# A two-layer SiLU network on one core: tile 0 of the first tokens transposed alone, slab 1 loaded from ScalarE's queue

## The chip, the core and the metric

The kernel runs on one core of one Trainium2 chip. The metric is device microseconds from the start to the end of one execution; a result is the median of several executions. Every duration below comes from the times, or from one profiled execution of the kernel.

The profile names the engines PE (TensorE, matrix products), PEld (TensorE's weight loads, which overlap the products), ACT (ScalarE), DVE (VectorE), POOL (GpSimd) and SP (SyncE). A "q" behind a name (SPq, ACTq) stands for that engine's instruction sequencer, which also issues DMAs.

## The reference

```python
B, S, D, F = 1, 2048, 640, 1728
x: (B, S, D)   w1: (D, F)   w2: (F, D)      # all bf16

def reference(x, w1, w2):
    h = jnp.einsum("bsd,df->bsf", x, w1)
    h = _silu(h)
    out = jnp.einsum("bsf,fd->bsd", h, w2)
    return out
```

## The kernel before

**Layout.** The first product needs the contraction dimension D on the 128 partitions. So `xT` holds x transposed: 5 tiles of D (`DT` = 5, 128 partitions each) by 2048 tokens. The transposing is done by the DMA (`dma_start_transpose`), and all transposes are issued from SP's queue. `w1s` holds w1 in 5 slabs, slab k being the 128 rows of D that belong to tile k. F = 1728 is 13 blocks of 128 columns (`FT` = 13) and a rest of 64. Tokens are worked in 4 chunks of 512 (`SCH`).

**First chunk.** In the first chunk data are still arriving, so the loops are turned inside out: for k = 0 to 4, for each of the first 8 blocks of F (`NO` = 8, one PSUM bank each), one product of slab k with tile k (lines 197 to 211). Each such product is a pair of matmuls of 64 output rows each (`step`, line 183) that run side by side in two halves of the array. PE's instruction stream thus waits in turn for tile 0 and slab 0 (line 199), the second part of slab 0 before block 5 (`NA` = 5, line 202), slab and tile 1, 2, 3 (line 205), slab and tile 4 (line 208). After that come blocks 8 to 12 of this chunk (lines 221 to 228, waiting for `ld_rest` and `ld_rest2`, the other columns of w1), the chunks 1 to 3 (lines 229 to 235, each waiting for its transposed tokens `ld_xc`), and the second product.

**Before the data.** PE starts with products of zeros: `first_dummies` (line 135) issues 13 products of 128 x 128 by 256 columns and then one pair of 64-row halves. They write PSUM that the first real product overwrites, and depend only on a memset of `z`.

**The order of the loads.** `early` (line 96) puts an instruction ahead of the barrier at the program's start, at the end of what its engine has there already; the order of the calls is thus the order on each queue. Before the change:

- SP: tiles 0 and 1 of chunk 0 in one transposing DMA (line 123); columns of blocks 5 to 7 of slab 0 (`ld_w1b`, line 148); slab 1; slab 2; tile 2; slab 3; tiles 3 and 4 in one DMA; slab 4; `ld_rest`; `ld_rest2`. Behind the barrier follow 15 transposing DMAs of one tile each for the chunks 1 to 3, and then w2.
- ScalarE: columns of blocks 0 to 4 of slab 0 (line 124, 160 KB), then the warm-up (lines 142 to 146): one SiLU on a small tile that makes the engine load its function table. It waits for POOL's memset of `warm`.

A slab's 8 blocks are 256 KB. The transposing DMAs are records of line 93 or 163, the loads of line 88, the matmuls of line 175 (and 132 for the products of zeros).

Of the kernel before, what the change touches and what calls it, by code (L numbers as in the profile page):

```python
# [9 lines left out]
def bass_standalone__dense_activation_silu__prompt_kernel(  # L10
# [13 lines left out]
    P = 128  # L24
# [5 lines left out]
    SCH = 512  # L30
# [8 lines left out]
    pe, act, dve, pool, sp = nc.tensor, nc.scalar, nc.vector, nc.gpsimd, nc.sync  # L39

    with ExitStack() as es:
# [18 lines left out]
        def sem(name):  # L60
            s = es.enter_context(nc.semaphore(name))
            count[s.name if hasattr(s, "name") else name] = 0
            return [s, 0]

        def tick(ins, s, n=1):
            ins.then_inc(s[0], n)
            s[1] += n
            return (s, s[1])

        def wait(eng, *points):  # L70
            for pt in points:
                if pt is None:
                    continue
                s, v = pt
                key = (id(eng), id(s))
                if seen.get(key, 0) < v:
                    eng.wait_ge(s[0], v)
                    seen[key] = v
# [6 lines left out]
        def load(eng, out_ap, in_ap):  # L85
            s = sem(f"s_ld{n_dma[0]}")
            n_dma[0] += 1
            return tick(eng.dma_start(out=out_ap, in_=in_ap), s, 16)

        def turned(c0, c1, k0, k1):  # L90
            s = sem(f"s_tr{n_dma[0]}")
            n_dma[0] += 1
            return tick(sp.dma_start_transpose(
                out=xT[:, k0:k1, c0:c1], in_=xf[c0:c1, k0 * P:k1 * P]), s, 16)

        ET = mybir.EngineType

        def early(emit, engine, arrived=True):
            n = len(nc.main_func.blocks[0].instructions)
            r = emit()  # L100
            lst = nc.main_func.blocks[0].instructions
            new = lst[n:]
            del lst[n:]
            at = next(
                i for i, ins in enumerate(lst)
                if ins.opcode == ("EventSemaphore" if arrived else "Drain") and ins.engine == engine
            )
            lst[at:at] = new
            return r
# [8 lines left out]
        def slab(eng, k, f0=0, f1=NO):  # L118
            return load(eng, w1s[:, k, f0 * P:f1 * P], w1_v[:, k, f0 * P:f1 * P])

        ld_w1 = {}
        ld_t = {}
        ld_t[0] = ld_t[1] = early(lambda: turned(0, SCH, 0, 2), ET.SP, False)
        ld_w1[0] = early(lambda: slab(act, 0, 0, NA), ET.Activation, False)
        p_z = early(lambda: tick(dve.memset(z[:, :], 0.0), s_dve), ET.DVE, False)  # L125

# [2 lines left out]
        def dummies(n, w):  # L129
            for _ in range(n):  # L130
                for c0 in range(0, P, w):
                    pe.matmul(ps[c0:c0 + w, 3, 0:HB], lhsT=z[:, 0:w], rhs=z[:, :],  # L132
                              start=True, stop=True)

        def first_dummies():
            wait(pe, p_z)
            dummies(13, P)
            dummies(1, HC)

        p_warm = early(lambda: tick(pool.memset(warm[:, :], 0.0), s_pool), ET.Pool, False)  # L140
# [4 lines left out]

        early(warm_up, ET.Activation, False)

        ld_w1b = early(lambda: slab(sp, 0, NA, NO), ET.SP, False)
        ld_w1[1] = early(lambda: slab(sp, 1), ET.SP, False)
        ld_w1[2] = early(lambda: slab(sp, 2), ET.SP, False)  # L150
        ld_t[2] = early(lambda: turned(0, SCH, 2, 3), ET.SP, False)
        ld_w1[3] = early(lambda: slab(sp, 3), ET.SP, False)
        ld_t[3] = ld_t[4] = early(lambda: turned(0, SCH, 3, DT), ET.SP, False)
        ld_w1[4] = early(lambda: slab(sp, 4), ET.SP, False)
# [42 lines left out]
        def opening():  # L197
            first_dummies()
            wait(pe, ld_t[0], ld_w1[0])
            for ft in range(NO):  # L200
                if ft == NA:
                    wait(pe, ld_w1b)
                part(0, ft, 0, SCH, start=True)
            for k in range(1, DT - 1):
                sweep(k, 0, SCH, ld_w1[k], ld_t[k])
# [202 lines left out]
```

## Time and profile before

| what | before |
|---|---|
| median of 3 runs | 124.61 us (124.4 to 124.67) |
| span of the profiled execution, first to last instruction | 123.84 us |
| PE busy | 121.3 us, 98% of the span |
| weight loads busy | 58.9 us |
| ACT busy | 38.8 us |
| DVE busy | 6.9 us |
| HBM read, written | 4.51 MB, 2.62 MB |
| granted TensorE clock in every stretch | 1.00 |

The span is 0.77 us shorter than the median time; that much lies around the first and the last recorded instruction. A busy PE is not a PE at its best rate: how fast it goes is read from the distance between the starts of successive products. A DMA has three moments: the issue (an instruction of SPq or ACTq with a duration of its own), the packets that the 16 DMA engines move, and the landing, when the last of the 16 semaphore increments has arrived. A row "x1, 3.8" among the DMA issues means 3.8 us from the start of the issue to the landing.

### The profile page before, as it was taken

Reading aid. Unit: us, or ns where it says so; the run is one execution under the profiler, and the core shown is the slowest. Engines: PE = TensorE matmul, PEld = TensorE weight load, DVE = VectorE, ACT = ScalarE, POOL = GpSimd, SP = SyncE. Lnnn points to the kernel's source line nnn. Section 1 sums busy time; section 2 is a strip of 40 time slices with the busy share of each in tenths; the row PEclk is TensorE's granted clock in tenths of the full one; section 3 lists DMA queues with packets and bytes.
Section 4 is the critical chain, followed back from the end, with each engine's and each line's share of the span. In section 5 each row is a group of like instructions: output and inputs, shape, how many; then the busy total and the mean of one; then the engine's idle time right before and its main releaser. Section 6 shows DMA issues by size and latency. Waiting matters only on the chain.

```text
span 123.8 us, 2298 instructions
## 1 busy us (share of the span) xinstructions
PE 121.3 (98%) x1056; PEld 58.9 (48%) x1057; DVE 6.9 (6%) x11; ACT 38.8 (31%) x67; POOL 0.3 (0%) x5
## 2 busy tenths in 40 slices
PE   8999999999999999999999999999999999999993
PEld 5345545545545545545544444444444444444452
DVE  0000000000000000000000022002200300222001
ACT  4000985555555555555530011001100200110110
POOL 0000000000000000000000000000000000000000
DMA  6999974554894000000000004302200220023112
GB/s 138 239 246 331 138 86 91 100 77 107 214 394 157 0 0 0 3 5 0 0 0 5 0 0 101 74 0 105 107 0 5 106 106 0 5 106 116 53 66 82
DMA packets 19625, 10.42 MB, mean 84 GB/s; under 512 B 13728, under 2 KB 19104, under 8 KB 19616
## 3 DMA queue, kind: packets, MB, share of 16 engines
q1 hardware_dynamic: 19472, 10.11, 34.1%
q10 hardware_dynamic: 144, 0.16, 0.6%
q8 instruction: 8, 0.13, 0.5%
q14 instruction: 1, 0.01, 0.0%
HBM read 4.51 MB, written 2.62 MB: 58 GB/s over the span
## 4 chain that ended last, share of the span: by engine, by line
PE 95%; DMA 3%; ACT 0%; issue 0%
PE ps L175 95%; DMA xT<-in_x_dram 3%; ACT o_sb L256 0%
## 5 line engine op out<-in xcount | busy, mean ns | idle before, releaser
L175 PE MATMUL ps<-xT,w1s 128*64 128x512 bf16 x540 | 59.6, 384 | 0.1
L175 PE MATMUL ps<-w2s,hT 64*128 64x512 bf16 (+3 forms) x376 | 46.0, 369 | 0.2 <-issue 0.2
L175 PEld LDWEIGHTS ps<-xT,w1s 128*64 128x64 bf16 x540 | 30.0, 111 | 29.6 <-issue 1.2
L179 ACT ACTIVATE hT<-ps 128x512 bf16<-128x512 f32 x52 | 30.0, 607 | 29.9 <-PE ps L175 29.9
L175 PEld LDWEIGHTS ps<-w2s,hT 64*128 64x128 bf16 (+1 forms) x377 | 21.0, 95 | 24.2 <-issue 0.2
L256 ACT CAST o_sb<-ps 128x512 bf16<-128x512 f32 (+1 forms) x9 | 5.0, 551 | 41.5 <-PE ps L175 41.5
L175 PE MATMUL ps<-hT,w2s 64*128 64x512 bf16 x104 | 11.7, 376 | 0.0
L175 PEld LDWEIGHTS ps<-hT,w2s 64*128 64x128 bf16 x104 | 5.0, 94 | 6.3 <-issue 0.4
L254 DVE CAST o_sb<-ps 128x512 bf16<-128x512 f32 (+1 forms) x8 | 5.4, 675 | 40.5 <-PE ps L175 40.5
L254 DVE CAST oT<-ps 128x512 bf16<-128x512 f32 x2 | 1.4, 692 | 74.2 <-PE ps L175 74.2
L256 ACT CAST oT<-ps 128x512 bf16<-128x512 f32 x2 | 1.2, 586 | 10.6 <-PE ps L175 10.6
L132 PE MATMUL ps<-z 128*128 128x256 bf16 (+1 forms) x15 | 3.3, 419 | 0.4 <-DVE z L125 0.4
L175 PE MATMUL ps<-w2t,hTt 64*128 64x512 bf16 (+2 forms) x17 | 2.9, 363 | 0.0
L132 PEld LDWEIGHTS ps<-z 128*128 128x128 bf16 (+1 forms) x15 | 1.9, 142 | 1.5 <-issue 0.4
L179 ACT ACTIVATE hTt<-ps 128x512 bf16<-128x512 f32 x2 | 1.2, 598 | 1.0 <-PE ps L175 1.0
L144 ACT ACT_TABLE_LOAD x1 | 1.3, 1283 | 0.5 <-issue 0.5
L175 PEld LDWEIGHTS ps<-w2t,hTt 64*128 64x128 bf16 x17 | 0.9, 94 | 1.1
L175 PE MATMUL ps<-hTt,w2t 64*128 64x512 bf16 x4 | 0.8, 376 | 0.0
L175 PEld LDWEIGHTS ps<-hTt,w2t 64*128 64x128 bf16 x4 | 0.2, 94 | 0.2
L144 ACT ACTIVATE warm<-warm 128x32 f32<-128x32 f32 x1 | 0.2, 229 | 0.0
L125 DVE MEMSET z<- 128x128 uint32 x1 | 0.2, 165 | 0.2 <-issue 0.2
L140 POOL MEMSET warm<- 128x32 f32 x1 | 0.1, 125 | 0.0
(4 smaller groups left out, 0.4 us busy)
## 6 DMA issues: line engine op xcount, KB each, us to landing
out_dram<-o_sb SPq DMA_DIRECT2D x15, 160.0 KB, 1.8
w2s<-in_w_dram SPq DMA_DIRECT2D x1, 1120.0 KB, 6.1
w1s<-in_w_dram SPq DMA_DIRECT2D x4, 256.0 KB, 4.1
w2s<-in_w_dram SPq DMA_DIRECT2D x1, 960.0 KB, 8.2
w1s<-in_w_dram SPq DMA_DIRECT2D x1, 560.0 KB, 7.0
w1s<-in_w_dram SPq DMA_DIRECT2D x1, 320.0 KB, 5.8
xT<-in_x_dram SPq DMA_TRANSPOSE x18, 3.7
w1s<-in_w_dram ACTq DMA_DIRECT2D x1, 160.0 KB, 2.7
```

Source lines behind the costliest of these rows:

```text
L125: p_z = early(lambda: tick(dve.memset(z[:, :], 0.0), s_dve), ET.DVE, False)
L132: pe.matmul(ps[c0:c0 + w, 3, 0:HB], lhsT=z[:, 0:w], rhs=z[:, :], start=True, stop=True)
L140: p_warm = early(lambda: tick(pool.memset(warm[:, :], 0.0), s_pool), ET.Pool, False)
L144: act.activation(out=warm[:, :], in_=warm[:, :], func=ACT.Silu)
L175: return pe.matmul(o, lhsT=l, rhs=r, start=start, stop=stop, skip_group_check=shared)
L179: r = tick(act.activation(out=out_ap, in_=in_ap, func=ACT.Silu), s_act)
L254: r = tick(dve.tensor_copy(out=out_ap, in_=in_ap), s_dve)
L256: r = tick(act.copy(out=out_ap, in_=in_ap), s_act)
```

## The change

```diff
-        ld_t[0] = ld_t[1] = early(lambda: turned(0, SCH, 0, 2), ET.SP, False)
+        ld_t[0] = early(lambda: turned(0, SCH, 0, 1), ET.SP, False)
         ld_w1[0] = early(lambda: slab(act, 0, 0, NA), ET.Activation, False)
...
         def first_dummies():
             wait(pe, p_z)
-            dummies(13, P)
+            dummies(11, P)
             dummies(1, HC)
...
         early(warm_up, ET.Activation, False)
 
+        ld_w1[1] = early(lambda: slab(act, 1), ET.Activation, False)
+
         ld_w1b = early(lambda: slab(sp, 0, NA, NO), ET.SP, False)
-        ld_w1[1] = early(lambda: slab(sp, 1), ET.SP, False)
+        ld_t[1] = ld_t[2] = early(lambda: turned(0, SCH, 1, 3), ET.SP, False)
         ld_w1[2] = early(lambda: slab(sp, 2), ET.SP, False)
-        ld_t[2] = early(lambda: turned(0, SCH, 2, 3), ET.SP, False)
         ld_w1[3] = early(lambda: slab(sp, 3), ET.SP, False)
```

SP's first DMA transposes tile 0 alone. Tiles 1 and 2 follow in one DMA behind the second part of slab 0. The load of slab 1 leaves SP's queue and stands in ScalarE's stream behind the warm-up. SP has three transposing DMAs for chunk 0 as before (1, 2 and 2 tiles in place of 2, 1 and 2). Two of the 13 full products of zeros are gone. What is computed, and everything behind the first chunk's loads, stays as it is.

## The prediction

> **What bounds the kernel now.** I read the chain of waits first.
>
> ```profile
> 0.00 3.78 DMA xT<-in_x_dram
> ...
> 3.82 106.78 PE ps L175 x706
> ```
>
> The columns are start, length, what. The first transposing DMA lands at 3.78 us; from 3.82 PE works without a hole that the chain shows to the end of the products. So the kernel is "landing of tile 0 plus the work of PE": only an earlier start, a better rate or a new hole on PE can move the end. Next the timeline (start, length, engine, what), to see the rate.
>
> ```profile
> 0.39 3.31 PE L132 MATMUL ps<-z 128*128 128x256 bf16 x15 [0.39 <-DVE z L125]
> 3.82 0.18 PEld L175 LDWEIGHTS ps<-xT,w1s 128*64 128x64 bf16 x4 [0.42 <-DMA xT<-in_x_dram]
> ...
> 5.53 0.18 PEld L175 LDWEIGHTS ps<-xT,w1s 128*64 128x64 bf16 x2 [0.25 <-DMA w1s<-in_w_dram]
> 5.96 0.18 PEld L175 LDWEIGHTS ps<-xT,w1s 128*64 128x64 bf16 x2 [0.25 <-issue]
> 6.30 23.64 PEld L175 LDWEIGHTS ps<-xT,w1s 128*64 128x64 bf16 x220 [0.17 <-issue]
> ...
> 23.56 0.60 ACT L179 ACTIVATE hT<-ps 128x512 bf16<-128x512 f32 x1 [0.48 <-PE ps L175]
> 24.64 0.60 ACT L179 ACTIVATE hT<-ps 128x512 bf16<-128x512 f32 x1 [0.48 <-PE ps L175]
> ```
>
> The reader is to see two rates. From 3.82 to 5.96 a pair of matmuls starts every 0.427 us (five steps in 2.14 us). From 6.30 on the idle gaps are gone, and a block of five pairs takes 24.64 - 23.56 = 1.08 us, 0.2155 us a pair. The step from 5.96 to 6.30 is a mixture: x at the slow rate with x/0.427 + (0.343 - x)/0.2155 = 1 gives x = 0.26, so the rate doubles at 6.22 us. (The granted clock is 1.00 in every stretch; the doubling shows in the spacing alone.) Five whole pairs and 0.6 of the sixth run slowly. Products of zeros keep PE occupied ahead of that, at 0.213 us each, half the later rate too.
>
> Then the queues, and what became of the first DMAs.
>
> ```profile
> 0.00 1.33 SPq L93 DMA_TRANSPOSE xT<-in_x_dram  x1
> 0.12 0.37 ACTq L88 DMA_DIRECT2D w1s<-in_w_dram  x1
> 0.52 1.28 ACT L144 ACT_TABLE_LOAD   x1 [0.52 <-issue]
> 1.39 1.54 SPq L88 DMA_DIRECT2D w1s<-in_w_dram  x3
> 1.82 0.23 ACT L144 ACTIVATE warm<-warm 128x32 f32<-128x32 f32 x1
> 2.97 1.16 SPq L93 DMA_TRANSPOSE xT<-in_x_dram  x1
> ...
> 4.79 1.24 SPq L93 DMA_TRANSPOSE xT<-in_x_dram  x1
> ```
>
> Issuing a transpose holds SP 1.2 to 1.3 us, whether for one tile (the row at 2.97) or two (0.00, 4.79). The rows of line 393, and windows of the DMAs (length, busy time of the engines with counts, granted clock, DMA share, GB/s) say the rest:
>
> ```profile
> L393 ACTq DRAIN  x1: 1475/1475/1475, 0.6 to 0.6; - x1
> ```
>
> ```profile
> 1.70:2.50 0.80, 0.80 (x6) 0.55 (x4) 0.00 (x0) 0.34 (x2) 0.00 (x0) 1.00 1.16 238
> 2.50:3.25 0.75, 0.75 (x4) 0.30 (x2) 0.00 (x0) 0.00 (x0) 0.00 (x0) 1.00 1.14 248
> 3.25:4.00 0.75, 0.63 (x5) 0.31 (x6) 0.00 (x0) 0.00 (x0) 0.00 (x0) 1.00 0.77 82
> ```
>
> ScalarE's sequencer stands at its drain at 0.6 us, while the table load runs to 1.80: it has handed the table load and the SiLU over and gone on. The windows show full engines to 3.25, then a weak stretch.
>
> **Part by part: tile 0 alone.** A tile of 512 tokens is 512 packets of 256 bytes, 131 KB. Of the 1,024 packets of the first DMA 497 have started by 2.5 us and 1,010 by 3.1 in the packet records; the second tile thus takes 0.6 us (131 KB at the 248 GB/s of the window above would be 0.53). Without it tile 0 would land at 3.78 - 0.60 = 3.18. Bounds: chunk 2 has a one-tile transpose on idle engines that lands 2.7 us after its issue, and two-tile 3.78 is the other end.
>
> **Slab 1 from ScalarE.** The diff puts it behind the warm-up, but the drain row says that the sequencer doesn't wait there: I expect the issue at about 0.6, ending at 1.0 (0.37 as for slab 0's part), not at 2.05. Its packets then stand right behind slab 0's 160 KB, which in the packet records are under way from 1.0 to 2.3 us, beside tile 0's (from 1.7). In 1.7 to 2.5 the two queues move about the same bytes. In the after slab 1 goes on taking a half of what tile 0 got alone in the last 0.1 to 0.2 us of its 0.8. Cost 0.1, with bounds 0 (issued at 2.05) and 0.67 (all of slab 1's 256 KB ahead of it, at the 390 GB/s of its better stretches). So tile 0 lands at 3.3, and PE starts at 3.34, 0.48 earlier.
>
> [...]
>
> **Two products of zeros fewer.** 2 x 0.213 = 0.43 us: the last pair, at 3.28 now, goes to 2.85 and its slot ends at 3.06. Cost nothing as long as it ends before tile 0 lands; left at 13 they would end at 3.49 and eat 0.15 of the gain. Slab 0's part lands at 2.86 and is no limit.
>
> **What an earlier start is worth.** It buys slow time. If the doubling stays at 6.22, PE does (6.22 - 3.34)/0.427 = 6.74 pairs before it and the other 1.26 of sweep 0 in 0.27: sweep 1 begins at 6.49 in place of 6.74. That is **-0.24**: half of 0.48. Bounds of this step: tile 0 at 2.7 would be capped by the zeros (3.06), -0.38; tile 0 at 3.78, nothing.
>
> **The queues behind.** SP loses one load of about 0.5 us, so its later issues stand 0.5 earlier (tile 1 and 2 at about 1.9, slab 2 at 3.1, slab 3 at 3.6, tiles 3 and 4 at 4.2, the chunk transposes at 7.5 in place of 8.1). What PE needs, and where it landed before: second part of slab 0 at 3.34 + 5 x 0.427 = 5.47 (5.24, behind two tiles, now one); slab 2 at 8.21 (6.6); slab 3 and tile 3 at 9.93 (8.2, 9.2); slab 4 at 11.66 (10.5); the rests at 13.38 and 15.54 (12.5, 14.1); chunk 1 at 18.78 (18.0). All hold even if nothing moves earlier. The one new deadline is tiles 1 and 2 at 6.49. Their DMA is issued at 1.9; the two-tile DMAs took 3.8 and 4.4 to land, which gives 5.7 to 6.3. Counting bytes: what had to be moved until tile 2 landed at 7.15 was the same plus slab 2 (256 KB), 0.67 us at 390 GB/s; 7.15 - 0.67 = 6.48. Both are in time, the second just; I take 6.1 and cost nothing. With that cover gone each 0.1 us late costs PE 0.1 at full rate. Bound: 7.15 itself, a hole of 0.66.
>
> **Sum.** 123.84 - 0.24 = 123.60 for the span, with the 0.77 around it **124.37** against the median 124.61, since the profiled execution plus 0.77 is that median.
>
> **Rivals.** (1) *The doubling comes with the work*: if it follows the first real product (2.40 us after 3.82) and not the clock on the wall, it moves along and the start counts in full: -0.48, 124.13. For it: it comes after the real data began. Against it: PE had been occupied since 0.39, which is what the zeros are for.
> (2) *Slab 1 holds tile 0 back*: with all of slab 1 ahead, 3.18 + 0.67 = 3.85 and PE starts at 3.89: +0.03, 124.64. For it the sharing row; against it that slab 1 queues behind slab 0's part until about 2.2, when most of tile 0 is through.
> (3) *Tiles 1 and 2 come late*, the case on the other side: sweep 1 stands where sweep 0 had been bought forward. The place is PE's wait of line 205 for k = 1; the price is landing minus 6.49, all at full rate; slower than before from a landing of 6.74 on. With 7.15 it is 0.66 - 0.24 = +0.42, 125.03. For it: the stretch 3.25 to 4.00 at 82 GB/s behind the first transpose, and another such behind the new one would fall on tile 1; against it the two estimates above.
> (4) *The doubling comes at another time.* If tile 0 lands late, PE stands idle from 3.06 and not from 3.49; should a longer gap put the doubling off by t, it costs 0.505 t, at 2 us late 1.0: 125.4. Against it: at 3.3 the gap is 0.28, less than the present 0.33.
> [...]
>
> **Chances.** Forecast 0.48, (1) 0.13, (2) 0.13, (3) 0.16, (4) 0.10. About 0.2%, 0.25 us, is what a measurement here tells from no change, and -0.24 stands on it: of the forecast I give 0.28 to faster and 0.20 to same, since tile 0 may land a little earlier than 3.3. (1) is faster; (2) is same for 0.08 and slower for 0.05; (3) is same for 0.03 and slower for 0.13; (4) slower. Faster 0.41, same 0.31, slower 0.28. The range reaches from 124.0 (rival 1 with tile 0 at 3.2) to 125.0 (rival 3 to its bound), leaving out most of (4) and little else; the forecast's own range is 124.2 to 124.6.
>
> **What will show it.** In the profile after: the first chain piece ends near 3.3 and not 3.78; ACTq has a second load issue near 0.6; slow pairs number nearly seven and weight loads lose their idle gaps near 6.2; sweep 1 starts near 6.5 with no wait for xT. A wait of PE for xT after 6 us is rival 3; a first piece at 3.8 rival 2; a change of spacing near 5.7 rival 1, one at 7 or later rival 4. Any hole on PE behind 20 us, or a rate other than 0.2155, would make the whole reading wrong.

## The result and the profile after

| | before | after |
|---|---|---|
| median | 124.61 us (124.4 to 125.11, 6 runs) | 126.29 us (124.98 to 126.78, 6 runs) |
| ratio to before | | 1.0126, 95% interval 1.0086 to 1.0165 |
| profiled execution: span | 123.84 us | 125.46 us |

The kernel became 1.3% slower; 124.37 with a gain was forecast. The runs of the changed kernel show time and span of one execution together: 126.78 with a span of 125.46, so 1.3 us lie around a span and not 0.77. The profiled execution of before was thus one of about 125.1 us, the upper end of its runs. Where a kernel has runs far above its own fastest, its ratio leaves them out, while medians and ranges count every run.

The chain of waits of the changed kernel (start, length, what):

```profile
0.00 4.62 DMA xT<-in_x_dram
4.62 0.04 issue
4.66 118.94 PE ps L176 x1041
```

The form is the one from before, a landing and then PE without a hole. But the landing, of half as much data, is at 4.62 us and not 3.78. The timeline of the changed kernel:

```profile
0.59 0.38 ACTq L88 DMA_DIRECT2D w1s<-in_w_dram  x1
...
1.83 0.23 ACT L144 ACTIVATE warm<-warm 128x32 f32<-128x32 f32 x1
...
4.66 0.18 PEld L176 LDWEIGHTS ps<-xT,w1s 128*64 128x64 bf16 x4 [1.68 <-DMA xT<-in_x_dram]
...
8.08 0.18 PEld L176 LDWEIGHTS ps<-xT,w1s 128*64 128x64 bf16 x2 [0.25 <-issue]
8.50 3.42 PEld L176 LDWEIGHTS ps<-xT,w1s 128*64 128x64 bf16 x32 [0.25 <-issue]
```

Slab 1 is issued at 0.59 us, long before the warm-up's SiLU runs at 1.83: "behind the warm-up" holds for the instruction stream alone. And the slow rate, the rows with idle gaps of 0.25 us ahead of the weight loads, now lasts until after 8.5 us. The step from 8.50 to the next pair is 0.283 us, which by the mixture of the two rates puts the doubling at 8.64.

**Where the 1.62 us of span went.** PE starts at 4.66 in place of 3.82: +0.84. In 4.66 to 8.64 it does (8.64 - 4.66)/0.427 = 9.3 slow pairs, before it was (6.22 - 3.82)/0.427 = 5.6; 3.7 pairs more at 0.427 - 0.2155 each are +0.78. Together 1.62, all of the difference. So there are two questions: why tile 0 lands so late, and why the rate doubles so late.

**Why tile 0 lands late: the trace.** Its 512 data packets have all started by 2.58 us, about as early as forecast. The packets that follow, in the view of the DMAs for two short stretches of the changed kernel (queue q1 is SP's, q10 ScalarE's; packets, MB, share of the engines):

```profile
DMA packets 80, 0.16 MB, mean 410 GB/s; under 512 B 0, under 2 KB 0, under 8 KB 80
## 3 DMA queue, kind: packets, MB, share of 16 engines
q10 hardware_dynamic: 80, 0.16, 107.4%
```

```profile
DMA packets 126, 0.08 MB, mean 264 GB/s; under 512 B 48, under 2 KB 111, under 8 KB 126
## 3 DMA queue, kind: packets, MB, share of 16 engines
q1 hardware_dynamic: 95, 0.05, 60.6%
q10 hardware_dynamic: 31, 0.03, 30.6%
```

The first stretch is 2.6 to 3.0 us: 80 packets, all of them of slab 1, none from SP's queue, although tile 0's data are through and only its small completion packets remain. These (4 bytes, in "under 512 B" with slab 1's own) go out in the second stretch, 3.0 to 3.3. The landing comes later still: the 16 increments of slab 1's semaphore arrive between 3.52 and 3.76, those of tile 0 only after them, from 3.77 to 4.62. In the run below that moves slab 1 alone the two sets overlap (4.00 to 4.65 and 4.18 to 4.85), so it is not that one DMA as a whole must end before the other.

### The profile page after: what moved, and what is told of

Same layout as the page of the kernel before. It is cut to its first block, busy times and chain, and to the rows that moved or that the text cites. A ratio compares the mean times of both kernels' runs of the same rounds, so it can differ in the third digit from the quotient of the medians.

```text
span 125.5 us, 2295 instructions
## 1 busy us (share of the span) xinstructions
PE 121.8 (97%) x1055; PEld 59.6 (47%) x1055; DVE 7.0 (6%) x11; ACT 38.8 (31%) x67; POOL 0.3 (0%) x5
## 4 chain that ended last, share of the span: by engine, by line
PE 95%; DMA 4%; ACT 0%; issue 0%
PE ps L176 95%; DMA xT<-in_x_dram 4%; ACT o_sb L257 0%
## 5 line engine op out<-in xcount | busy, mean ns | idle before, releaser
L176 PE MATMUL ps<-xT,w1s 128*64 128x512 bf16 x540 | 60.4, 388 | 1.4 <-DMA xT<-in_x_dram 1.4
L176 PEld LDWEIGHTS ps<-xT,w1s 128*64 128x64 bf16 x540 | 30.9, 112 | 30.7 <-issue 2.2
```

The costliest lines, as they stand in the source:

```text
L176: return pe.matmul(o, lhsT=l, rhs=r, start=start, stop=stop, skip_group_check=shared)
```

## The experiments

Theory A: slab 1's run of packets on ScalarE's queue gets in between tile 0's data and its completion. Rival B: tile 0 alone is late by itself. For the doubling, theory H: the stretch in which PE idles puts it off. Rival C: each missing product of zeros does. A sweep is the eight products of one slab with its tile; sweep 0 is the first.

**Slab 1 back on SP.**

```diff
-        ld_w1[1] = early(lambda: slab(act, 1), ET.Activation, False)
         ld_w1b = early(lambda: slab(sp, 0, NA, NO), ET.SP, False)
+        ld_w1[1] = early(lambda: slab(sp, 1), ET.SP, False)
         ld_t[1] = ld_t[2] = early(lambda: turned(0, SCH, 1, 3), ET.SP, False)
```

> The changed kernel with slab 1 back on SP's queue, between the second part of slab 0 and the transpose of tiles 1 and 2; tile 0 alone and 11 products of zeros stay. Theory A (slab 1 on ScalarE's queue holds back tile 0's completion: in the changed kernel tile 0's last packet starts at 2.55 us, its completion packets only at 3.05 to 3.25 when slab 1's packets are through, and it lands at 4.62): tile 0 lands near 3.2, the first real product starts near 3.25, the rate doubles near 6.2, and the median is 124.2 to 124.6, or up to 0.4 more if tiles 1 and 2 are now late for sweep 1. Theory B (tile 0 alone is late by itself, whatever stands on ScalarE's queue): tile 0 still lands after 4.2, the rate doubles after 8 us, median about 126.3. Theory C (the missing products of zeros are what puts off the doubling): tile 0 early, yet the doubling near 8.6 us and a median near 125.4.

Measured: 124.79 us (124.5 to 125.22) against 124.25 on that chip, ratio 1.0021 (1.0001 to 1.0042). Tile 0 lands at 3.03; its issue row, and the DMAs of this run in 2.2 to 2.4 us:

```profile
xT<-in_x_dram SPq DMA_TRANSPOSE x1, 3.0
```

```profile
DMA packets 171, 0.04 MB, mean 199 GB/s; under 512 B 171, under 2 KB 171, under 8 KB 171
## 3 DMA queue, kind: packets, MB, share of 16 engines
q1 hardware_dynamic: 171, 0.04, 93.2%
```

Here the first completion packets go out among the last data, 0.8 us earlier than in the changed kernel. A holds, B falls. The doubling comes at 3.2 us and not 8.64 with the same 11 products, which speaks against C; as the doubling comes anywhere from 3.1 to 8.64 us in the profiles of this case, one profile can't settle it, but the twelve runs with 11 products further down do. What is left shows in PE's timeline of this run:

```profile
3.07 1.96 PE L175 MATMUL ps<-xT,w1s 128*64 128x512 bf16 x16
6.22 5.13 PE L175 MATMUL ps<-xT,w1s 128*64 128x512 bf16 x44 [1.19 <-DMA xT<-in_x_dram]
```

PE begins at 3.07, at the full rate almost at once, finishes sweep 0 and stands until tiles 1 and 2 land at 6.09. That is rival 3 of the prediction, and here it eats the whole gain.

**Slab 1 on ScalarE's queue alone.**

```diff
-        ld_w1[1] = early(lambda: slab(sp, 1), ET.SP, False)
+        ld_w1[1] = early(lambda: slab(act, 1), ET.Activation, False)
```

> The kernel before, with one part of the change alone: slab 1 goes from SP's queue to ScalarE's, behind the warm-up. Tiles 0 and 1 stay in one transpose, 13 products of zeros stay. Theory A: the landing of the first transpose moves from 3.78 us to 4.3 to 4.9, the idle time of PE ahead of the first real product grows from 0.33 to over 0.8 us, and the kernel is slower by 0.3 us (start alone) to 1.7 us (start, and the doubling one step later). Theory B: nothing moves, the landing stays within 0.2 us of 3.78 and the median within 0.3 us of the one before.

Measured: 125.07 to 127.52 us, median of all ten runs 127.0, against 124.25, ratio 1.0099 (1.0059 to 1.0139). The first transpose lands at 4.85:

```profile
0.00 4.85 DMA xT<-in_x_dram
```

One part of the change, in the kernel before, makes the delay. The runs fall into two groups, four of 125.1 to 125.6 and six of 126.8 to 127.5. The upper one is 2.5 to 3.3 us above 124.25, more than the 0.3 to 1.7 us expected. The profiled run is the fastest and at the full rate when real work starts at 4.89, so no trace shows the rate in the upper group.

**More products of zeros.**

```diff
-            dummies(11, P)
+            dummies(18, P)
```

> The changed kernel with 18 products of zeros in place of 11, the last pair ending near 4.6 us, when tile 0 lands in the changed kernel. If the idle stretch of PE (2.85 or 3.06 to 4.66 us) is what puts off the doubling of the rate from 6.22 to 8.64 us, the doubling comes back to 6.0 to 6.6 us, the first real product stays at 4.7 us, and the median falls by 0.7 to 0.9 us, to 125.4 to 125.6. If the doubling follows the first real product (some 4 us behind it) or its own clock on the wall, the median stays at 126.3.

Measured: 124.84 us (124.4 to 125.2) against 124.25, ratio 1.0027 (1.0005 to 1.0049). Weight loads of this run:

```profile
0.39 3.14 PEld L132 LDWEIGHTS ps<-z 128*128 128x128 bf16 x18 [0.39 <-DVE z L125]
4.22 8.77 PEld L176 LDWEIGHTS ps<-xT,w1s 128*64 128x64 bf16 x84 [0.38 <-DMA xT<-in_x_dram]
```

Tile 0 still lands late (4.18), but no run is above 125.2. In this run the rate doubles at 3.1 us, inside the products of zeros, earlier than the 6.0 to 6.6 us expected, so they end sooner than planned, yet the real work starts at the full rate. The median is below the 125.4 to 125.6 of the forecast. As one profile shows one doubling, it is the twelve times, and not this one profile, that carry the reading. The changed kernel's 1.0126 falls to 1.0027 by filling the idle stretch alone: most of the loss goes with that stretch, by H through the rate, the smaller part with the landing.

**Slab 1 issued after the warm-up's end.**

```diff
+            return tick(act.activation(out=warm[:, :], in_=warm[:, :], func=ACT.Silu), s_act)
...
+            wait(act, p_up)
+            return slab(act, 1)
```

> The changed kernel in which ScalarE's sequencer waits for the end of the warm-up's SiLU before it issues slab 1, so at about 2.1 us in place of 0.6; its packets then start near 2.9 us, behind tile 0's last one (2.55). Theory A: tile 0's completion packets go out at about 2.6, tile 0 lands at 3.1 to 3.3, the doubling comes near 6.2, slab 1 lands near 5 and is in time for sweep 1; median 124.2 to 124.6. Theory B: tile 0 lands after 4.2, median near 126.3.

Measured: median 126.14 us (124.92 to 128.5), ratio 1.0089 (1.0053 to 1.0124). Tile 0 lands at 3.01 as A says, but the time was forecast wrong. PE's timeline of this run, and its windows with GB/s at the end:

```profile
3.07 2.94 PE L180 MATMUL ps<-xT,w1s 128*64 128x512 bf16 x16
7.74 1.49 PE L180 MATMUL ps<-xT,w1s 128*64 128x512 bf16 x12 [1.73 <-DMA xT<-in_x_dram]
```

```profile
3.25:4.00 0.75, 0.75 (x8) 0.26 (x4) 0.00 (x0) 0.00 (x0) 0.00 (x0) 1.00 0.86 159
4.00:5.00 1.00, 1.00 (x8) 0.46 (x6) 0.00 (x0) 0.00 (x0) 0.00 (x0) 1.00 0.94 172
```

Issued at 2.1 us, slab 1 falls among the transpose of tiles 1 and 2, and both DMAs land late: slab 1 at 7.40 and the two tiles at 7.60, though these are issued at 1.92 as in the changed kernel, where they land at 5.68. Sweep 1 waits for them. While both are under way the engines move 159 to 172 GB/s. Whether the sharing makes the rate low is not shown: in the changed kernel SP's queue alone moves 161 GB/s from 3.3 to 4.4 us. Why the runs spread as far as 128.5 us is not shown either; the profiled one took 126.19.

**Products of zeros taken from the kernel before, no DMA changed.**

```diff
-            dummies(13, P)
+            dummies(11, P)      # and, in another run, 8
```

> The kernel before with 11 products of zeros in place of 13, no DMA changed: PE idles from 3.06 to 3.82 us, 0.76 us in place of 0.33. [...] Rival C (every missing product of zeros puts the doubling off): median up by 0.2 us or more in every run, with no runs in the lower half of the range of before.

> The kernel before with 8 products of zeros in place of 13, no DMA changed: PE idles from 2.42 to 3.82 us, 1.4 us, as long as in the changed kernel (1.6), and tile 0 still lands at 3.78. Theory H: the runs fall into two groups, a small one in the range of the kernel before (124.0 to 124.6, doubling before the idle stretch) and a large one 1 to 2 us above it, 125.5 to 127, with the doubling at 7 to 9.5 us; median up by 1 to 2 us. If the loss in the changed kernel comes from the late transfer alone and the idle stretch has nothing to do with the clock, the median stays within 0.3 us of the one before.

Measured with 11: 124.45 us against 124.31, ratio 1.0010 (0.9988 to 1.0033), eleven runs from 123.94 to 125.15 and one of 126.32. With 8: 125.66 (125.0 to 126.63), ratio 1.0126 (1.0086 to 1.0165). Five missing products, with no transfer touched, cost as much as the whole change. In the profiled executions the first transpose landed at 3.63 (11 products) and 3.42 us (8), so PE idled for 0.62 and 1.04 us, less than the 0.76 and 1.4 expected. By the times, a stretch of 0.6 to 0.8 us is nearly free (0.14 us) and one of 1.0 to 1.4 is not (1.35 us), which fits H. But the late doubling that H expects with 8 was not seen: the one profile is of the fastest execution, its rate doubles at 6.3 us, and its span, 123.68, is no longer than before's 123.84. So the changed kernel's profile is the only one that shows a late doubling. The small fast group that I expected with 8 didn't show in six runs. Three profiles with the DMAs of before thus have the first landing at 3.42, 3.63 and 3.78 us; the 1.2 to 1.6 us that slab 1 adds are well beyond that spread. Weight loads of the profiled execution with 8:

```profile
0.38 1.41 PEld L132 LDWEIGHTS ps<-z 128*128 128x128 bf16 x8 [0.38 <-DVE z L125]
3.46 0.19 PEld L175 LDWEIGHTS ps<-xT,w1s 128*64 128x64 bf16 x4 [1.13 <-DMA xT<-in_x_dram]
6.36 6.59 PEld L175 LDWEIGHTS ps<-xT,w1s 128*64 128x64 bf16 x62 [0.15 <-issue]
```

**Half of slab 1 on ScalarE's queue.**

```diff
-        ld_w1[1] = early(lambda: slab(act, 1), ET.Activation, False)
+        ld_w1[1] = early(lambda: slab(act, 1, 0, NO // 2), ET.Activation, False)
...
         ld_t[1] = ld_t[2] = early(lambda: turned(0, SCH, 1, 3), ET.SP, False)
+        ld_w1c = early(lambda: slab(sp, 1, NO // 2, NO), ET.SP, False)
...
-                sweep(k, 0, SCH, ld_w1[k], ld_t[k])
+                sweep(k, 0, SCH, ld_w1[k], ld_t[k], ld_w1c if k == 1 else None)
```

> The changed kernel with only blocks 0 to 3 of slab 1 (128 KB) on ScalarE's queue; blocks 4 to 7 stand on SP's queue behind the transpose of tiles 1 and 2, and PE waits for both before sweep 1. Theory A (tile 0's completion packets wait until the other queue's run of packets is through): with half as much in front the completion packets go out near 2.7 us (2.3 with none, 3.05 to 3.25 with the whole slab) and tile 0 lands at 3.3 to 3.8 us (3.0 with none, 4.2 to 4.6 with the whole); the median lies between, 124.6 to 125.8. If a load on ScalarE's queue holds it back whatever its size (a cost of the queue, not of its bytes), tile 0 lands at 4.2 or later.

Measured: 125.2 us (124.92 to 126.05), ratio 1.0083 (1.0054 to 1.0111). The issue row of tile 0:

```profile
xT<-in_x_dram SPq DMA_TRANSPOSE x1, 3.5
```

The completion packets go out at 2.5 to 2.8. With nothing, half and all of slab 1 in between tile 0 lands at 3.0, 3.5 and 4.2 to 4.6: the delay goes with the bytes, not with the queue. The median holds a second loss: sweep 1 waits for the other half, which lands at 6.64.

**Slab 1 issued at 1.4 us, between SP's first two transposes.**

```diff
+        p_pad = early(lambda: tick(dve.memset(pad[:, :], 0.0), s_dve), ET.DVE, False)
...
+            wait(act, p_pad)
+            return slab(act, 1)
```

> The changed kernel in which ScalarE's sequencer waits for a longer memset of VectorE (960 words a partition, ending near 1.4 us by 128 words in 0.165) before it issues slab 1: after SP has issued tile 0, before it issues tiles 1 and 2. Theory A: slab 1's packets come behind tile 0's completion packets (2.2 to 2.5 us), tile 0 lands at 3.0 to 3.2 us, PE starts near 3.1 without an idle stretch, slab 1 lands before tiles 1 and 2 (near 5.5), sweep 1 waits for these some 0.7 us when the rate has doubled early; median 123.6 to 124.3, at or below the kernel before. If the memset ends before 1.0 us, slab 1 still falls on the completion packets and the landing is 3.5 to 4.6; if the issue queues behind that of tiles 1 and 2, slab 1 and these land at 7 or later as with the issue at 2.1, median 125 or more.

Measured: 124.53 us (124.31 to 124.98) against 124.31, ratio 1.0020 (1.0001 to 1.0040). Its timeline, ScalarE's queue and then PE:

```profile
1.37 0.34 ACTq L89 DMA_DIRECT2D w1s<-in_w_dram  x1
```

```profile
3.15 8.11 PE L182 MATMUL ps<-xT,w1s 128*64 128x512 bf16 x60
```

The issue three quarters of a microsecond later, timed by a memset on VectorE, is the only difference from the changed kernel: tile 0 lands at 3.11, PE works from 3.15 without a hole, and all but 0.2% of the loss is gone. But it is no gain, and lies above the forecast of 123.6 to 124.3. In this profile the rate doubles at 6.1 us, close to the 6.22 of before, and there the span is 0.4 shorter (123.44 against 123.84). Its fastest run, however, is 124.31 where before reaches 123.89. What takes the gain when the rate doubles early is open, as no profile of this kernel with an early doubling was taken. Two landings of this profile would bind then. The second part of slab 0 lands at 5.07, and the weight loads wait for it even here:

```profile
5.11 0.36 PEld L182 LDWEIGHTS ps<-xT,w1s 128*64 128x64 bf16 x4 [0.49 <-DMA w1s<-in_w_dram]
```

Tiles 1 and 2, together, land at 5.89. Before, sweep 1 needs slab 1, which landed at 5.88, 5.75 and 5.34 in the profiles with 13, 11 and 8 products, so that landing alone doesn't decide it.

**Slab 1 on ScalarE's queue with 20 products of zeros; all of slab 0 from ScalarE's queue.**

```diff
 # slab 1 on ScalarE's queue in the kernel before, and
-            dummies(13, P)
+            dummies(20, P)
```

> The kernel before with slab 1 on ScalarE's queue, as in the earlier run with that one part, and 20 products of zeros in place of 13, which reach past 4.8 us at the slow rate (less at the full one). In that earlier run tiles 0 and 1 landed at 4.85 us and the times lay between 125.1 and 127.5. If the upper part of them is the idle stretch of PE (1.4 us), the runs above 126 vanish and the median falls to 124.9 to 125.5; what is left against the kernel before is the late landing itself. If the upper part comes from the transfers, runs above 126 stay.

Measured: 125.61 us (125.32 to 125.94) against 124.16, ratio 1.0122 (1.0086 to 1.0158). None of the four runs is above 126, which fits the idle stretch as the cause of the upper group; four runs are too few to show it, and against the lower group of 125.1 to 125.6 nothing is won. The median is 0.1 above the forecast: tile 0 landed at 5.11 here. At the full rate, which this profile has from 3.8 us on, a late start counts in full: PE starts at 5.15 in place of 3.82, 1.3 us, of the 1.4 us that the median is above 124.16.

```diff
 # slab 1 at 1.4 us as above, and all of slab 0 from ScalarE's queue
-        ld_w1[0] = early(lambda: slab(act, 0, 0, NA), ET.Activation, False)
+        ld_w1[0] = early(lambda: slab(act, 0), ET.Activation, False)
...
-        ld_w1b = early(lambda: slab(sp, 0, NA, NO), ET.SP, False)
...
-                if ft == NA:
-                    wait(pe, ld_w1b)
 # or, in another run, the second part as a load of its own behind the first
+        ld_w1b = early(lambda: slab(act, 0, NA, NO), ET.Activation, False)
```

> Tile 0 alone, slab 1 on ScalarE's queue from 1.4 us on, and in addition all of slab 0 in one load on ScalarE's queue (no second part on SP), so that SP issues tiles 1 and 2 right behind tile 0, at 1.3 us. Theory A: slab 0's longer run of packets (256 KB in place of 160) holds tile 0's completion to about 2.6, it lands at 3.2 to 3.4; tiles 1 and 2 land at 5.0 to 5.5 in place of 5.9, slab 1 at 5 to 5.5. Median 123.8 to 124.2, 0.1 to 0.5 below the kernel before. If slab 1's packets fall among the transpose of tiles 1 and 2 as with the issue at 2.1, these land at 6.5 or later and the median is 125 or more.

> As the run with all of slab 0 in one load, but the two parts of slab 0 stay two loads, both on ScalarE's queue one behind the other (160 KB at 0.1 us, 96 KB at 0.6 us). Tile 0 lands at 3.1 to 3.4 us, the second part of slab 0 at 3.2 to 3.6, tiles 1 and 2 at 5.0 to 5.5; median 123.8 to 124.2, within 0.2 us of the run with one load.

Measured: 125.02 us (124.77 to 125.6) against 124.16, ratio 1.0072 (1.0044 to 1.0101), and with two loads 124.92 (124.71 to 125.21), ratio 1.0063 (1.0039 to 1.0087). Both forecasts of 123.8 to 124.2 missed; what came is the other case that the first of them names (6.5 us or later, 125 or more). Tile 0 lands at 3.54 and 3.71, tiles 1 and 2 at 6.69 and 6.59, though issued 0.6 us earlier: slab 1's packets now run beside this transpose (2.5 to 5.2 us and 2.8 to 5.1), as in the run with the issue at 2.1.

## Why the prediction was wrong

- **Tile 0 alone: right.** 3.18 us was worked out; without slab 1 on the other queue it lands at 3.0. (The packet records give 497 packets by 2.6 us and 1,010 by 3.16, not 2.5 and 3.1; the second tile's 0.6 us becomes 0.56.)
- **Slab 1's issue at 0.6: right** (0.59), and SP's early issues to within 0.25 us; the chunk transposes began at 8.04 and not at 7.5.
- **"Cost 0.1, with bounds 0 and 0.67": the step that failed.** It counted how many of slab 1's bytes go ahead of tile 0's data. The landing came later as the completion packets did. Without slab 1 there these go out from 2.2 us on and tile 0 lands at 3.03, with half of it from 2.5 and at 3.5. With all of it they come behind slab 1's run, from 3.05, and the landing behind slab 1's, at 4.62 in place of 3.3. Even the bound, 3.85, was too low. Rival 2 had the place, not the price. (Nor do the two queues move "about the same bytes" in 1.7 to 2.5 us: it is 0.11 MB on SP's queue and 0.08 on ScalarE's.) The runs show the order in time (80 packets of slab 1 with none of SP's beside them, tile 0's increments from 3.77 behind slab 1's last at 3.76) and that the delay goes with slab 1's bytes; by what mechanism is not shown.
- **"Two products of zeros fewer: cost nothing as long as it ends before tile 0 lands": wrong by its own condition.** The products of zeros cover a late landing. With tile 0 at 4.62 PE idled from 3.06 for 1.6 us, and the doubling went from 6.22 to 8.64. The runs with 18 products, and with 8 in the kernel before, show that filling or emptying the stretch takes most of the loss away (ratio 1.0027) or makes it (1.0126). This was rival 4, with a chance of 0.10. Its price of 0.505 a microsecond should be 1 - 0.2155/0.427 = 0.495: 2.42 us late cost 1.20 of the 1.62, and the start 0.84 later, at 0.505, the other 0.42. It follows from rival 2, and should not have stood as a case of its own.
- **The doubling at 6.22 as a constant: wrong.** Without an idle stretch of 1 us or more it came at 3.1 (18 products), 3.2 (slab 1 back on SP), 4.6 (half of slab 1), 5.2 (issue after the warm-up), 5.3 (11 products before), 6.1 (issue at 1.4), and 6.4 (all of slab 0 in one load). The gain of a start 0.5 us earlier is a half of it only where the doubling falls late. No run here shows what sets the moment. I had another one as rival 4 and kept the constant.
- **"With the 0.77 around it": wrong.** It joined the span of a late execution of before, of about 125.1 us, to the median of others. With 1.3 us around it, a span of 123.60 is 124.9. So the -0.24 was worked out for one of the slowest executions of the kernel before.
- **Tiles 1 and 2: not tested in the changed kernel**, where sweep 1 begins after they have landed (5.68). In three experiments with an early start they (6.09, 7.60) or slab 1's second half (6.64) were what sweep 1 waited for, and in the last two runs, for a shorter time, they again. Rival 3 is the next bound, not an accident.

## What to carry to other kernels

Here a small urgent DMA landed at 3.03 us with its completion packets from 2.2 us on, and at 4.62 us with them from 3.05, behind slab 1's run on the other queue. So look at what any other queue has ready in the 1 us after its last data packet, not only at what shares its bandwidth. ScalarE's sequencer issued slab 1 at 0.59 us, while the table load ran to 1.81, and at 1.37 with a wait for a memset that ended at 1.34: a delay there has to be written as a wait. Filler work ahead of the doubling of TensorE's rate should reach close to the latest moment at which data can arrive; here 0.6 to 0.8 us short of it was nearly free (0.14 us) and 1.0 to 1.6 us was not (1.35 us with 8 products, 1.68 us in the changed kernel, where the landing was late as well). When early work runs at a rate that changes, and the moment differs between profiles (3.1 to 8.64 us here), judge a change of the start by many runs, and by both an early and a late such moment.

## What the runs showed beside this

Five products of zeros, about 1.1 us of work on nothing, are worth 1.35 us in the median of a kernel of 124. Once the rate had doubled, a hole did not bring the slow rate back here: after the waits of 1.19 us (slab 1 back on SP) and 1.73 us (issue after the warm-up) PE goes on at 0.215 to 0.216 us a pair. A transpose of tiles 1 and 2 issued at 1.92 us landed 3.8 us later where slab 1's data were through by then, and 5.7 us later where they ran beside it. And a transpose of one tile lands 3.0 to 3.1 us after the start of its issue while slab 0's 160 KB run beside it, little more than the 2.7 to 3.1 us that the least delayed one-tile transposes of the later chunks take.
